# Three steps of a fused attention and two-layer kernel: the weights' conversion pieces issued behind the copies of the first sums

## The chip, the cores and the metric

The kernel runs on one core of a Trainium2 chip. Its time is that of the device, in microseconds (us), from the first to the last instruction of the one core with what lies around them. Three runs of the kernel before gave 1049.48, 1050.41 and 1051.83 us; their median, 1050.41 us, is the time to compare with.

The engines are named as in the profile: PE multiplies matrices (PEld loads its stationary operand), ACT is the scalar engine, DVE the vector engine, POOL the GpSimd engine, SP the queue that issues the DMAs. Each engine takes its instructions strictly in the order in which they were issued to it, and waits where an instruction needs something that is not there yet.

## The reference

Clustered attention over 2 batches, 8 heads and 768 positions gives `x` of 1536 rows by 512. Then come two feed-forward layers; the change lies in the first of them:

```
def _moe_ref(x, w_in, w_out):            # x 1536x512, w_in 512x2048, w_out 2048x512
    h = x @ w_in
    g = np.where(h > 0.0, h, 1.0 * (np.exp(np.minimum(h, 0.0)) - 1.0))
    return (g @ w_out).astype(np.float32)

def _moe2_ref(x, domain_probs, w1, w2):  # four experts, w1 4x512x1024, w2 4x1024x512
    p = domain_probs / (domain_probs.sum(-1, keepdims=True) + 1e-09)
    out = np.zeros((N, D), dtype=np.float32)
    for e in range(E):
        h = np.maximum(x @ w1[e], 0.0)
        out += p[:, e:e + 1] * (h @ w2[e])
    return out.astype(np.float32)
```

## The kernel before

**Products in parts.** Every fp32 operand is kept as a high and a low part, and a product is three matmuls: high by high, high by low, low by high. A weight of layer one has to be converted into these two parts before its first use.

**Steps of layer one.** The 2048 hidden columns are cut into 16 chunks of 128, and the 1536 rows into three blocks (tb) of 512. `steps` lists pairs of a block and a chunk. The chunks come in groups of 2, 4, 5 and 5, and within a group all chunks are done for block 0, then for block 1, then for block 2. So steps 0 to 5 take chunks 0 and 1 (0, 1 for block 0, 2, 3 for block 1, 4, 5 for block 2), and steps 6 to 9 take chunks 2, 3, 4 and 5 for block 0. Chunk 2 is met first in step 6, chunk 3 in step 7, chunk 4 in step 8, chunk 5 in step 9; chunk 6 only in step 18.

**What a step does.** `emit_G1(s)` is the first product: 12 matmuls (L753) into PSUM bank `h0` or `h1` (by the parity of s), then ELU: ACT makes `r` (L760, L761), DVE makes `gg` from `r` and the bank (L762), and POOL makes its high and low part `gh`, `gl` (L763, L764). The bank is free for the first product of step s + 2 when L762 of step s has read it. `emit_G2(s)` is the second product: 12 matmuls (L923), three for each of four 128-column sums. The four sums of a group of chunks stay in PSUM until the group ends; then ACT copies them out if it is the block's first group (L939, four copies, at the end of steps 1, 3 and 5) and DVE adds them to the accumulator otherwise (L941). The sums rotate through five PSUM banks: in the step that opens the next group, the first sum has a free bank, and the second sum's three matmuls wait for the first of the four copies.

The loop runs two steps ahead: iteration s issues `emit_G1(s + 2)`, then `emit_G2(s)`. PE thus goes G1(s+2), G2(s), G1(s+3), G2(s+1), and so on.

**Conversion of a chunk.** `w_split(n)` is a generator; each call of `tick` moves every running generator on by one piece. The pieces of one chunk, with one yield behind each group:

| piece | ACT | DVE | POOL |
|---|---|---|---|
| 1 | L710 (abs of the high word, to `wa`) | | |
| 2 | L716 (sign, to `wsg`) | L712, L715 | |
| 3 | | L718 (joins the low word) | |
| 4 | L722 | | |
| 5 | | L724 (times `wsg`) | |
| 6 | L726 (the high part, `wh`) | | L729 (the low part, `wl`) |

There is one buffer `wsg` for all chunks, so L716 of a chunk waits until L724 of the chunk before has read it. The raw words lie in two buffers `st`; the DMA for a chunk waits until L718 and L716 of the chunk two before are done. `tick` is called twice in an iteration of layer one, with 2s ahead of the products and with 2s + 1 behind them. A new chunk starts every 3 ticks (chunks 2 to 5) or every 4, so two chunks are under way at a time.

What sets the order on each engine is only the order in which this loop calls things. In what follows, "step s" also names iteration s of the loop.

Of the kernel before, what the change touches and what calls it, by code (L numbers as in the profile page):

```python
# [46 lines left out]
def kernel(  # L47
# [538 lines left out]
    groups, chunks, steps = [], [], []  # L586
# [37 lines left out]
    def w_load(n, raw=None, half=None):  # L624
        ly, f = chunks[n]
        if raw is None:
            t = moe_p["st"].tile([128, 2, 512, 2], I32, tag="st", name="st")
            raw = [t[:, 0], t[:, 1]]
            st_t[n] = t
        if ly == 1:  # L630
            for i, a in enumerate(raw):
                if half == 1 or i == 1:
                    src = w_out.bitcast(I32)[f * 128:(f + 1) * 128, :]
                    sp.dma_start(out=a.rearrange("p f t -> p (f t)"), in_=src)
                else:
                    src = w_in.bitcast(I32)[:, f * 256:(f + 1) * 256].rearrange("(k p) f -> p k f", p=128)
                    sp.dma_start(out=a.rearrange("p (k f) t -> p k (f t)", k=KD), in_=src)
            if half is not None:
                st_t[n] = raw[0]
        else:  # L640
            e, f = divmod(f, F2 // 256)
            f = slice(f * 256, (f + 1) * 256)
            a, b = (x.bitcast(F32).rearrange("p f t -> p (f t)") for x in raw)
            sp.dma_start(
                out=a.rearrange("p (k f) -> p k f", k=KD), in_=w1[e][:, f].rearrange("(k p) f -> p k f", p=128)
            )
            sp.dma_start(
                out=b.rearrange("p (c d) -> p c d", c=2), in_=w2[e][f, :].rearrange("(c p) d -> p c d", p=128)
            )
# [41 lines left out]
    def w_split(n, tmp=None, half=None):  # L691
        if chunks[n][0] == 2:
            yield from w2_split(n)
            return
        a = st_t.pop(n)
        if n not in w_t:
            w_t[n] = w_tiles(n)
        h, l = w_t[n]
        if half is not None:
            h, l = h[:, half], l[:, half]  # L700

        small = tmp is not None
        a32, sg = tmp if small else [gtile(("qh", "kl", "kh")[n % 3], "wa", [128, 2, 512], I32), gtile("ql", "wsg", [128, 2, 512], I32)]
        at = (slice(None),) * (len(a.shape) - 1)
        hi, lo = a[at + (1,)], a[at + (0,)]
        x, sg = a32.bitcast(F32), sg.bitcast(F32)

        act.activation(out=x, in_=hi.bitcast(F32), func=AF.Abs)  # L710
        yield
        dve.tensor_scalar(x, x, LOW, TOP, ALU.max, ALU.min)  # L712
        if small:
            yield
        dve.tensor_scalar(a32, a32, 3, 0x40000000, ALU.logical_shift_left, ALU.bitwise_xor)  # L715
        act.activation(out=sg, in_=hi.bitcast(F32), func=AF.Sign)  # L716
        yield
        dve.scalar_tensor_tensor(  # L718
            out=a32, in0=lo, scalar=29, in1=a32, op0=ALU.logical_shift_right, op1=ALU.bitwise_or
        )  # L720
        yield
        act.activation(out=x, in_=x, func=AF.Abs)  # L722
        yield
        dve.tensor_tensor(out=x, in0=x, in1=sg, op=ALU.mult)  # L724
        yield
        act.activation(out=h, in_=x, func=AF.Copy)  # L726
        if small:
            yield
        pool.tensor_tensor(l, x, h.bitcast(F32), ALU.subtract)  # L729
        yield  # L730

    def moe():
# [172 lines left out]
        def emit_G2(s, ms=range(4)):  # L905
            ly, tb, n, opens, closes, first, final = steps[s]
            if opens and 0 in ms:
                for m in range(4):
                    a_ps[m] = ps_a.tile([128, 512], F32, tag="a", name="a")
            if first and opens and 0 in ms:  # L910
                acc[tb] = accp.tile([128, 4, 512], F32, tag=f"acc{tb}", name="acc")
            for m in ms:
                ps, t, col = a_ps[m], acc[tb][:, m], slice(m * 128, (m + 1) * 128)
                ops = []
                for i, (gh, gl) in enumerate(g_t[s]):
                    if ly == 1:
                        wh, wl = w_t[n]
                        ops += [(wh[:, 1, col], gh), (wh[:, 1, col], gl), (wl[:, 1, col], gh)]
                    else:
                        wh, wl = (z[:, i] for z in w_t[n][1])  # L920
                        ops += [(gh[:, col], wh), (gh[:, col], wl), (gl[:, col], wh)]
                for i, (x, y) in enumerate(ops):
                    pe.matmul(ps, lhsT=x, rhs=y, start=(opens and i == 0), stop=(closes and i == len(ops) - 1))  # L923
                if ly == 1 or not closes:
                    continue
                i = 4 * tb + m
                e = chunks[n][1] // (F2 // 256)
                pr = prob[:, i, e:e + 1]
                if first:
                    dve.tensor_scalar(out=t, in0=ps, scalar1=pr, scalar2=None, op0=ALU.mult)  # L930
                else:
                    dve.scalar_tensor_tensor(out=t, in0=ps, scalar=pr, in1=t, op0=ALU.mult, op1=ALU.add)  # L932
                if final:
                    bb, tt = divmod(i, T)
                    sp.dma_start(out=out[bb * S:(bb + 1) * S, :].rearrange("(p t) d -> t p d", t=T)[tt], in_=t)
            if ly == 1 and closes:
                for m in ms:
                    if first:
                        act.activation(out=acc[tb][:, m], in_=a_ps[m], func=AF.Copy)  # L939
                    else:  # L940
                        dve.tensor_tensor(out=acc[tb][:, m], in0=a_ps[m], in1=acc[tb][:, m], op=ALU.add)  # L941
                if final:
                    x2_gen[tb] = x2_make(tb, acc[tb])
                    if tb < NB - 1:
                        going.append(x2_gen[tb])
                    else:
                        next(x2_gen[tb])

        def probs():
            t = tp.tile([128, B * T, 1], F32, tag="xs", name="ps")  # L950
            for b in range(B):
                sp.dma_start(
                    out=prob[:, b * T:(b + 1) * T, :],
                    in_=domain_probs[b * S:(b + 1) * S, :].rearrange("(p t) e -> p t e", t=T),
                )
            dve.tensor_reduce(out=t, in_=prob, axis=AX.X, op=ALU.add)
            dve.tensor_scalar(out=t, in0=t, scalar1=1e-9, scalar2=None, op0=ALU.add)
            dve.reciprocal(out=t, in_=t)
            dve.tensor_tensor(out=prob, in0=prob, in1=t.to_broadcast([128, B * T, E]), op=ALU.mult)


        NS1 = NS - NB * NP
# [24 lines left out]
        def tick(t, k=1):  # L987
            for n in start.get(t, ()):
                w_gen2[n] = w_split(n)
                going.append(w_gen2[n])  # L990
            for _ in range(k):
                going[:] = [it for it in going if next(it, 0) is None]
            for n in load_at.get(t, ()):
                w_load(n)
# [5 lines left out]
        def ready(s):  # L1000
            for it in (x2_gen[steps[s][1]], w_gen2[steps[s][2]]):
                for _ in it:
                    pass

        for s in range(-LAG, NS):


            nxt = s + (1 if s >= NS1 else LAG)
            q = None
            if s < NS1:  # L1010
                tick(2 * s)
            if nxt < NS1:
                emit_G1(nxt)
            elif nxt < NS and s != NS1 - 1:
                ready(nxt)
                q = quad_early(nxt)
            if s >= 0:
                emit_G2(s, (0,) if q else range(4))
            if s < NS1:
                tick(2 * s + 1)  # L1020
            if q:
                quad_late(nxt, *q)
                if s >= NS1:
                    tick(2 * s, 3)
                    tick(2 * s + 1, 2)
                emit_G2(s, (1, 2, 3))
            g_t.pop(s, None)
            if s == 12:
                probs()

    attention()
    moe()


# [28 lines left out]
```

## Time and profile before

| what | value |
|---|---|
| median of three runs | 1050.41 us (1049.48 to 1051.83) |
| the profiled execution, its time | 1049.74 us |
| the profiled execution, its span | 1048.0 us |
| PE matmul busy | 1030.3 us, 98% of the span |
| DVE, ACT, POOL busy | 735.5, 524.4, 393.3 us |
| mean granted TensorE clock | 0.997 |

The span runs from the first to the last instruction; the other 1.7 us of the execution's time lie around it. A matmul's busy time in the profile is longer than its share of the array, since matmuls overlap: 12 matmuls of 512 columns take 2.72 us from the first's start to the next group's start. So what a stall costs is read from the starts of matmuls, not from PE's busy share. Layer one begins at 269.58 us of the span (first L753) and its last L753 ends at 525.2 us; steps 0 to 9 lie between 275 and 330 us.

### The profile page before, as it was taken

The numbers are of one execution on the slowest core, as the hardware profiler recorded it, in microseconds if no ns is written. First come the engines' busy times: TensorE is split into PE (matmuls) and PEld (weight loads), VectorE is DVE, ScalarE is ACT, GpSimd is POOL, SyncE is SP. The second block draws the span as 40 slices with busy tenths as digits, with TensorE's granted clock in tenths as the row PEclk, the third lists the DMA queues.
The fourth block names the chain that finished last, engine by engine and source line by source line (L and its number), as shares of the span: only waits on it lengthen the run. The fifth ranks groups of instructions, "written<-read, shape, count | busy, mean of one in ns | idle before, by whom it ended". The sixth has DMA issues, their size and how long they took to land.

```text
span 1048.0 us, 16483 instructions
## 1 busy us (share of the span) xinstructions
PE 1030.3 (98%) x6272; PEld 920.8 (88%) x6272; DVE 735.5 (70%) x1248; ACT 524.4 (50%) x1081; POOL 393.3 (38%) x394
## 2 busy tenths in 40 slices
PE   8999999999999999999999999999999999999998
PEld 7989999989877888888888898999999898989997
DVE  6999999898689674326576765666666767666665
ACT  4989999888776563324443332233332333332331
POOL 2888888989678766344641000000000000000000
PEclk8999999999999999999999999999999999999999
DMA  7846654430323221010002101111101111001003
GB/s 171 200 104 159 143 133 113 114 91 12 136 96 122 81 95 67 1 41 1 0 1 81 41 1 41 41 41 42 40 2 41 41 41 41 15 27 41 1 1 120
DMA packets 61790, 67.53 MB, mean 64 GB/s; under 512 B 29008, under 2 KB 47440, under 8 KB 61712
## 3 DMA queue, kind: packets, MB, share of 16 engines
q1 hardware_dynamic: 61712, 66.49, 22.4%
q8 instruction: 49, 0.80, 0.3%
q14 instruction: 29, 0.24, 0.1%
HBM read 43.08 MB, written 3.15 MB: 44 GB/s over the span
## 4 chain that ended last, share of the span: by engine, by line
PE 82%; DVE 8%; ACT 4%; POOL 3%; issue 2%; DMA 0%; DVEq 0%; POOLq 0%; ACTq 0%; SPq 0%
PE a L923 35%; PE h L773 23%; PE h L753 10%; PE x L445 4%; PE tps L412 4%; PE s L364 2%; PE s L367 2%; POOL p L400 2%; DVE pl L433 2%; DVE nm L373 1%; DVE wa L718 1%; PE qkps L199 1%; ACT ph L425 1%; PE lps L239 1%; PE lps L240 1%
## 5 line engine op out<-in xcount | busy, mean ns | idle before, releaser
L773 PEld LDWEIGHTS h<-x,w1op 128*128 128x128 f32 x2016 | 257.5, 191 | 10.2 <-ACT r L784 1.2
L773 PE MATMUL h<-x,w1op 128*128 128x256 f32 x2016 | 261.2, 285 | 1.0 <-ACT r L784 1.0
L923 PE MATMUL a<-w2op,gh 128*128 128x512 f32 x768 | 238.5, 392 | 0.0
L923 PEld LDWEIGHTS a<-w2op,gh 128*128 128x128 f32 x768 | 138.1, 188 | 23.8
L932 DVE SCALAR_TENSOR_TENSOR acc<-a,prob,acc 128x512 f32<-128x512 f32 x180 | 129.7, 747 | 40.2 <-PE a L923 40.2
L923 PE MATMUL a<-w2op,gl 128*128 128x512 f32 x384 | 149.9, 390 | 0.0
L753 PE MATMUL h<-xT,wh 128*128 128x512 f32 x384 | 118.5, 390 | 0.6 <-DVE gg L762 0.6
L400 POOL TENSOR_SCALAR p<-e,sm 128x768 f32<-128x768 f32 x96 | 89.0, 933 | 40.8 <-DVE sm L394 31.0
L762 DVE SCALAR_TENSOR_TENSOR gg<-r,h 128x512 f32<-128x512 f32 x48 | 32.9, 685 | 96.5 <-ACT r L761 75.3
L373 DVE TENSOR_REDUCE nm<-s 128x1 f32<-128x768 f32 x96 | 90.8, 946 | 2.8 <-PE s L367 2.6
L382 ACT ACTIVATE e<-s,nm 128x768 f32<-128x768 f32 x96 | 86.6, 902 | 4.4 <-POOL p L400 3.2
L412 PE MATMUL tps<-ident,p 128*128 128x128 f32 x576 | 83.8, 277 | 3.2 <-DVE pl L433 3.0
L753 PEld LDWEIGHTS h<-xT,wh 128*128 128x128 f32 x384 | 71.9, 188 | 16.1 <-DVE gg L762 1.5
L784 ACT ACTIVATE r<-h 128x256 f32<-128x256 f32 x48 | 18.4, 384 | 134.8 <-PE h L773 134.8
L923 PEld LDWEIGHTS a<-w2op,gl 128*128 128x128 f32 x384 | 72.2, 188 | 15.6
L433 DVE TENSOR_TENSOR pl<-tps,ph 128x512 fp32r<-128x512 f32 x112 | 76.2, 683 | 6.6 <-ACT ph L425 5.0
L760 ACT ACTIVATE r<-h 128x512 f32<-128x512 f32 x48 | 28.6, 596 | 97.7 <-PE h L753 96.9
L445 PE MATMUL x<-ph,v 128*128 128x256 f32 x288 | 76.5, 298 | 0.1
L923 PE MATMUL a<-gh,wh 128*128 128x512 f32 x192 | 75.0, 391 | 1.0 <-ACT acc L939 0.9
L763 POOL TENSOR_SCALAR gh<-gg 128x512 fp32r<-128x512 f32 x48 | 41.0, 854 | 92.0 <-DVE gg L762 91.1
L923 PE MATMUL a<-gl,wh 128*128 128x512 f32 x192 | 74.9, 390 | 0.0
L753 PE MATMUL h<-xT,wl 128*128 128x512 f32 x192 | 74.8, 389 | 0.0
(152 smaller groups left out, 1948.4 us busy)
## 6 DMA issues: line engine op xcount, KB each, us to landing
st<-in_moe_w_dram SPq DMA_DIRECT2D x32, 512.0 KB, 4.3
st<-in_moe_w_in_dram SPq DMA_DIRECT2D x14, 512.0 KB, 3.7
st<-in_moe_w_out_dram SPq DMA_DIRECT2D x14, 512.0 KB, 4.6
QA<-qh SPq DMA_DIRECT2D x32, 192.0 KB, 3.6
nq<-in_q_dram SPq DMA_DIRECT2D x16, 192.0 KB, 3.8
nk<-in_k_dram SPq DMA_DIRECT2D x16, 192.0 KB, 3.9
nv<-in_v_dram SPq DMA_DIRECT2D x8, 384.0 KB, 3.9
QB<-ql SPq DMA_DIRECT2D x16, 192.0 KB, 3.9
```

The source lines that it names most:

```text
L373: dve.tensor_reduce(out=m_t[w][:, i:i + 1], in_=s_t[HALF * w + i][:, :, 0:384], axis=AX.XY, op=ALU.max, negate=True)
L382: act.activation(out=e, in_=s_t.pop(u)[:, :, 0:384], func=AF.Exp, bias=m_t[w][:, i:i + 1], accum_out=e_t[w][0][:, i:i + 1])
L400: pool.tensor_scalar(p, e_t[w][1 + i].rearrange("p a b -> p (a b)"), e_t[w][0][:, i:i + 1], 1.0, ALU.mult, ALU.mult)
L412: pe.transpose(ps[:, x, :], p_t[w][i][:, c * 128:(c + 1) * 128], ident)
L433: dve.tensor_tensor(out=l, in0=ps, in1=h.bitcast(F32), op=ALU.subtract)
L445: pe.matmul(x_t[w], lhsT=v2[j][:, r, c, :], rhs=t[:, :, c, :], start=(c == 0 and t is ph[w]), stop=(c == T - 1 and t is pl[w]),)
L753: pe.matmul(ps, lhsT=w[:, 0, f], rhs=x, start=(kk == 0 and i == 0), stop=(kk == KD - 1 and i == 2))
L762: dve.scalar_tensor_tensor(out=gg, in0=r, scalar=-1.0, in1=ps, op0=ALU.add, op1=ALU.max)
L763: pool.tensor_scalar(gh, gg, 1.0, 0.0, ALU.mult, ALU.add)
L773: pe.matmul(ps, lhsT=w[wz][kk], rhs=x[xz][:, kk], start=(start and kk + i == 0), stop=(stop and kk == 1 and i == 2), skip_group_check=True,)
L923: pe.matmul(ps, lhsT=x, rhs=y, start=(opens and i == 0), stop=(closes and i == len(ops) - 1))
L932: dve.scalar_tensor_tensor(out=t, in0=ps, scalar=pr, in1=t, op0=ALU.mult, op1=ALU.add)
```

## The change

In a tuple of `steps`, entry 4 says that the step closes its group of chunks and entry 5 that the group is the first. Both hold in steps 1, 3 and 5 alone, the steps whose second products end with the four copies. In these three iterations `tick(2 * s)` moves from ahead of both products to behind the second product and its copies; `tick(2 * s + 1)` follows it at once.

```diff
@@ -1007,7 +1007,9 @@
 
             nxt = s + (1 if s >= NS1 else LAG)
             q = None
-            if s < NS1:
+
+            late = 0 <= s < NS1 and steps[s][4] and steps[s][5]
+            if s < NS1 and not late:
                 tick(2 * s)
             if nxt < NS1:
                 emit_G1(nxt)
@@ -1016,6 +1018,8 @@
                 q = quad_early(nxt)
             if s >= 0:
                 emit_G2(s, (0,) if q else range(4))
+            if late:
+                tick(2 * s)
             if s < NS1:
                 tick(2 * s + 1)
             if q:
```

PE's and SP's orders stay as they are, up to buffer numbers. On ACT, DVE and POOL pieces of chunks 3 to 6 change places with the work of the first products of steps 3, 5 and 7 and with the copies.

ACT in iterations 3 and 4, before. `wh_4575` is the high part of chunk 4; the L710 and L716 ahead of it belong to chunk 5, the L722 behind it to chunk 5 and the L710 behind that to chunk 6. The first pair L760, L761 is that of step 5, the second that of step 6, and the copies are those of step 3.

```order
L722 ACTIVATE wa<-wa 128x1024
L710 ACTIVATE wa<-st 128x1024
L716 ACTIVATE wsg<-st 128x1024
L760 ACTIVATE r<-h 128x512
L761 ACTIVATE r<-r 128x512
L939 ACTIVATE acc<-a 128x512 x4
L726 ACTIVATE wh_4575<-wa 128x1024
L722 ACTIVATE wa<-wa 128x1024
L710 ACTIVATE wa<-st 128x1024
L760 ACTIVATE r<-h 128x512
```

And with the change (`wh_4613` is now the high part of chunk 4):

```order
L722 ACTIVATE wa<-wa 128x1024
L710 ACTIVATE wa<-st 128x1024
L760 ACTIVATE r<-h 128x512
L761 ACTIVATE r<-r 128x512
L939 ACTIVATE acc<-a 128x512 x4
L716 ACTIVATE wsg<-st 128x1024
L726 ACTIVATE wh_4613<-wa 128x1024
L722 ACTIVATE wa<-wa 128x1024
L710 ACTIVATE wa<-st 128x1024
L760 ACTIVATE r<-h 128x512
```

L716 of chunk 5 has gone from ahead of step 5's L760 to behind the copies. What follows it on ACT, down to step 6's L760, keeps its order.

DVE in iterations 3 and 4, before. `gg_4644`, `gg_4693` and `gg_4743` belong to steps 4, 5 and 6; `wa_4577` is chunk 4, `wa_4670` chunk 5.

```order
L762 SCALAR_TENSOR_TENSOR gg_4644<-r_4643,h_4628 128x512
L724 TENSOR_TENSOR wa_4577<-wa_4577,wsg_4578 128x1024
L712 TENSOR_SCALAR wa_4670<-wa_4670 128x1024
L715 TENSOR_SCALAR wa_4670<-wa_4670 128x1024
L762 SCALAR_TENSOR_TENSOR gg_4693<-r_4692,h_4677 128x512
L718 SCALAR_TENSOR_TENSOR wa_4670<-st_4571,wa_4670 128x1024
L762 SCALAR_TENSOR_TENSOR gg_4743<-r_4742,h_4727 128x512
```

And with the change (`gg_4689` is step 5's, `wa_4615` is chunk 4):

```order
L762 SCALAR_TENSOR_TENSOR gg_4644<-r_4643,h_4628 128x512
L762 SCALAR_TENSOR_TENSOR gg_4689<-r_4688,h_4673 128x512
L724 TENSOR_TENSOR wa_4615<-wa_4615,wsg_4616 128x1024
L712 TENSOR_SCALAR wa_4670<-wa_4670 128x1024
L715 TENSOR_SCALAR wa_4670<-wa_4670 128x1024
L718 SCALAR_TENSOR_TENSOR wa_4670<-st_4571,wa_4670 128x1024
L762 SCALAR_TENSOR_TENSOR gg_4743<-r_4742,h_4727 128x512
```

L724 of chunk 4 and L712 and L715 of chunk 5 now stand behind step 5's L762, right ahead of chunk 5's L718.

POOL in iterations 4 to 6, the difference. The first L764 is that of step 5; the pairs L763, L764 behind it are those of steps 6 and 7; `wl_4576` (now `wl_4614`) is chunk 4's low part, `wl_4669` chunk 5's.

```order
 L764 TENSOR_TENSOR gl<-gg,gh 128x512
-L729 TENSOR_TENSOR wl_4576<-wa,wh_4575 128x1024
+L729 TENSOR_TENSOR wl_4614<-wa,wh_4613 128x1024
+L763 TENSOR_SCALAR gh<-gg 128x512
+L764 TENSOR_TENSOR gl<-gg,gh 128x512
 L763 TENSOR_SCALAR gh<-gg 128x512
 L764 TENSOR_TENSOR gl<-gg,gh 128x512
 L729 TENSOR_TENSOR wl_4669<-wa,wh_4668 128x1024
-L763 TENSOR_SCALAR gh<-gg 128x512
-L764 TENSOR_TENSOR gl<-gg,gh 128x512
```

Chunk 5's L729 stood between the pairs of steps 6 and 7; it now stands behind both. (In iteration 5 its L726 has gone behind step 7's L760, L761 and step 5's copies on ACT, and chunk 6's L718 behind step 7's L762 on DVE.)

## Rows read from the trace of the kernel before

**Rows 1.** Waits, 265 to 345 us: who waited for whom, us, times, longest.

```profile
ACT wa L722 <- DVE wa L718: 8.8, 6, 2.8
...
PE a L923 <- ACT acc L939: 0.9, 1, 0.9
...
PE h L753 <- DVE gg L762: 0.6, 1, 0.6
```

**Rows 2.** Chain that ended last, 255 to 345 us: start, us, what.

```profile
315.82 3.01 PE h L753 x12
...
321.64 2.72 PE h L753 x12
```

**Rows 3.** Timeline of PE, steps 3 and 4: start, us, line, out<-in, count [idle before].

```profile
294.09 0.39 PE L923 MATMUL a<-gh,wh 128*128 128x512 f32 x1
...
300.39 0.40 PE L923 MATMUL a<-gh,wl 128*128 128x512 f32 x1
301.71 0.50 PE L923 MATMUL a<-gh,wh 128*128 128x512 f32 x1 [0.92 <-ACT acc L939]
```

**Rows 4.** Timeline of PE, in step 9's first product and at step 7's second.

```profile
316.40 0.39 PE L753 MATMUL h<-xT,wl 128*128 128x512 f32 x1
...
318.67 0.39 PE L923 MATMUL a<-gh,wh 128*128 128x512 f32 x1
```

**Rows 5.** Timeline of ACT, around steps 1, 3 and 4.

```profile
285.03 1.06 ACT L722 ACTIVATE wa<-wa 128x1024 f32<-128x1024 f32 x1 [1.01 <-DVE wa L718]
...
297.38 1.15 ACT L710 ACTIVATE wa<-st 128x1024 f32<-128x1024 f32 x1
298.87 1.16 ACT L716 ACTIVATE wsg<-st 128x1024 f32<-128x1024 f32 x1 [0.33 <-DVE wa L724]
299.93 0.58 ACT L760 ACTIVATE r<-h 128x512 f32<-128x512 f32 x1
...
301.08 2.04 ACT L939 ACTIVATE acc<-a 128x512 f32<-128x512 f32 x4
...
303.94 1.08 ACT L722 ACTIVATE wa<-wa 128x1024 f32<-128x1024 f32 x1
...
305.90 0.62 ACT L760 ACTIVATE r<-h 128x512 f32<-128x512 f32 x1
```

**Rows 6.** Timeline of DVE, around steps 1 to 5.

```profile
288.97 1.34 DVE L724 TENSOR_TENSOR wa<-wa,wsg 128x1024 f32<-128x1024 f32 x1
290.23 1.11 DVE L712 TENSOR_SCALAR wa<-wa 128x1024 f32<-128x1024 f32 x1
291.38 1.67 DVE L715 TENSOR_SCALAR wa<-wa 128x1024 int32<-128x1024 int32 x1
293.07 3.31 DVE L718 SCALAR_TENSOR_TENSOR wa<-st,wa 128x1024 int32<-128x1024 int32 x1
...
301.88 1.22 DVE L718 SCALAR_TENSOR_TENSOR wa<-st,wa 128x1024 int32<-128x1024 int32 x1
307.29 0.69 DVE L762 SCALAR_TENSOR_TENSOR gg<-r,h 128x512 f32<-128x512 f32 x1 [4.19 <-ACT r L761]
...
310.17 1.67 DVE L715 TENSOR_SCALAR wa<-wa 128x1024 int32<-128x1024 int32 x1
```

**Rows 7.** Timeline of POOL, around steps 0 to 7.

```profile
283.95 1.53 POOL L763 TENSOR_SCALAR gh<-gg 128x512 fp32r<-128x512 f32 x1 [2.05 <-DVE gg L762]
285.56 1.30 POOL L764 TENSOR_TENSOR gl<-gg,gh 128x512 fp32r<-128x512 f32 x1
286.81 2.41 POOL L729 TENSOR_TENSOR wl<-wa,wh 128x1024 fp32r<-128x1024 f32 x1
...
292.54 2.76 POOL L729 TENSOR_TENSOR wl<-wa,wh 128x1024 fp32r<-128x1024 f32 x1
...
321.98 3.39 POOL L729 TENSOR_TENSOR wl<-wa,wh 128x1024 fp32r<-128x1024 f32 x1
```

**Rows 8.** Windows: busy us of each engine, then PEclk, the granted clock.

```profile
10.00:20.00 10.00, 9.72 (x57) 9.05 (x57) 5.03 (x19) 2.27 (x7) 1.00 (x1) 0.66 0.96 210
```

## Prediction

> **What bounds the kernel now.** I read the table of waits first, then the chain that ended last, then the timelines of the engines where the three steps lie. From 321.64 us on the chain is PE alone, one product in 2.72 us [rows 2]: nothing that the change touches can gain there. The stretch to look at ends at that point. The waits in it that stop PE are small: 0.9 us for a copy (L939) and 0.6 us for a `gg` (L762); the long one, 8.8 us in six pieces, is ACT's L722 waiting for DVE's L718, which stops PE only through what is queued behind it [rows 1]. PE's starts give the whole loss: step 3's second product starts at 294.09 and step 7's at 318.67, which is 24.58 us for eight products that take 8 x 2.72 = 21.76, so 2.82 us are lost, and 0.25 us more up to 321.64 (2.97 us for one product) [rows 2 to 4]. Together 3.07 us, 0.29% of the time: more than that the change cannot gain, and 0.2% (2.1 us) is about what a measurement can tell from no change.
>
> One of the stalls is the copies': step 4's second sum starts at 301.71 where the matmul ahead of it started at 300.39; at 2.72 / 12 = 0.227 us a matmul that is 1.09 us late [rows 3]. The reader should see on ACT why: step 5's L760 could read its bank when step 3's second product began, at 294.09, but it started at 299.93, behind L716 of chunk 5, which waited for DVE's L724; the copies came at 301.08 [rows 5].
>
> **A price needed first: DVE against POOL.** The same L718 takes 1.22 us once and 3.31 us another time [rows 6]. The long one began at 293.07, while POOL's L729 ran from 292.54 to 295.30 [rows 7], and ended at 296.38, 1.08 us behind it. L729 too takes 2.41 or 3.39 us [rows 7]. So in this kernel conversion pieces of DVE and POOL do not overlap: the second waits for the first and then does nearly its whole work. The Trainium skill says so in a rule (SBUF — State Buffer, "SBUF: two separate sides"): the port pair that the vector engine and GpSimd share is an exclusive lock, held for the whole instruction, and the loser blocks fully. By that rule L718 costs its 3.31 us wherever a POOL piece is ahead of it; by the short row alone it would cost 1.22, and the sum below would come out 2.1 us smaller, at +4.0. The rule speaks against this change, since it puts DVE pieces where POOL is at work; the rows agree with it.
>
> **Step 1: nothing.** L722 of chunk 3 and L710 of chunk 4 go behind L760, L761 and the copies. Before, ACT stood idle for 1.01 us up to 285.03, waiting for DVE [rows 5]. L760 and L761 of step 3 fill that hole, the copies (2.04 us less their overlap, 1.9) end at about 287.1, and L722 ends at 288.15, so L724 of chunk 3 can start 0.8 us earlier than its 288.97. But POOL's L729 of chunk 2 runs to 289.22 (286.81 + 2.41) [rows 7], and both L724 end 1.08 us behind that, at 290.3 [rows 6]. From there the engines stand as before.
>
> **Step 3: the copies' stall goes, a longer one comes.** Without L716 of chunk 5 ahead of it, step 5's L760 follows L710, which takes about 1.0 us of ACT's queue (L722 and L710 together 303.94 to 305.90, 1.96): 297.38 + 1.0 = 298.4 instead of 299.93. The copies come as much earlier, 299.5 instead of 301.08, and PE's second sum, which followed the first copy by 0.63 us, is no longer held. Gain: 1.09 us and about 0.1 us that PE needs to start again, 1.2 us.
>
> The price is on DVE. L762 of step 5 follows its L760 by 1.39 us (305.90 to 307.29) [rows 5, 6], so at 299.8, and L724 of chunk 4 now stands behind it: 300.4, ending at 301.6 with 1.22 us. Before it had ended at 298.87, where L716 was released [rows 5]. Behind L724 come L712, L715 and L718 of chunk 5. The same four met POOL's L763, L764 and L729 in the same order for chunks 3 and 4: L724 ended at 290.31 and L718 at 296.38, 6.07 us later [rows 6, 7]. Here L763 and L764 of step 5 and L729 of chunk 4 (its L726 follows L716 on ACT, at about 302.6) are the same company, so L718 of chunk 5 ends at 301.6 + 6.07 = 307.7; before, 301.88 + 1.22 = 303.10. That is 4.6 us later.
>
> Behind it on ACT wait L722 of chunk 5, L710 of chunk 6 and then step 6's L760, which PE needs: 307.7 + 1.96 = 309.7; L762 at 311.1, done at 311.75. It frees the bank for step 8's first product. When would PE come for it? From the second sum at 301.71 there are 9 + 12 + 12 = 33 matmuls up to it, 7.5 us, and 0.1 for the restart: 309.3 before; without the copies' stall 308.1. So PE stands for about 3.5 us; less the 1.2 us gained, step 3 alone costs 2.3 us at this place.
>
> **Step 5: the weights of chunk 5 come too late.** Step 6's L762 is at 311.1 instead of 307.29. The DVE pieces behind it (L724 of chunk 5, L712 and L715 of chunk 6) ended 4.55 us after its start (310.17 + 1.67 - 307.29) [rows 6], so now at 315.65, and step 7's L762, now right behind them, ends at 316.3. POOL does L763 and L764 of step 7 next: 1.53 and 1.30 us with L718 of chunk 6 in their way, as for step 2 (283.95 to 286.81) [rows 7], from 316.4 to 319.3. Only then comes L729 of chunk 5, which stood ahead of them before. DVE's L724 of chunk 6 is there too by then (on ACT, L726 of chunk 5 and L722 of chunk 6 follow the copies), so I take the long duration, 3.39: 322.6. The third matmul of step 9's first product is the first to read `wl` of chunk 5. It started at 316.40 [rows 4]; now at 322.5. No more is added behind it: chunks 2 to 5 are then all converted and chunk 6 is met nine steps later, and the rest of the product and the next restart as they did before.
>
> SP's DMAs keep their order; their waits (L718, L716 of the chunk two before) move with the pieces, and the next load, chunk 6's, still waits for L718 and L716 of chunk 4, which do not move.
>
> **Sum.** 322.5 - 316.4 = +6.1 us: it holds the gain at the copies and the stall at step 8 already, since both lie ahead. The profiled execution took 1049.74 us, 0.67 below the median, so 1055.8 by it and 1056.5 by the median; I say 1056.0. Bounds: with the short L718 (1.22, DVE getting its turn ahead of L729: 305.6, 2.1 us earlier) and the short L729 (2.41, 1.0 earlier) +3.0 remains, 1052.7 to 1053.4. With POOL's L763 and L764 both some 0.3 us longer and slower restarts of PE, +6.9, 1056.6 to 1057.3.
>
> **The rivals.**
> *The conversion has room (faster).* Had it, all 3.07 us could come back: 1046.7 to 1047.3. It decides at L718 of chunk 5: it must end by 304.1 for PE not to wait at step 8, 1.0 us later than before, and L729 of chunk 5 by 313.3 (316.40 - 3.07). For it speaks that L718 has taken 1.22 us; against it, that even so it ends at 305.6, and that POOL's two pieces of step 7 now stand ahead of L729. Chance 0.04.
> *The pieces are hidden after all (no change).* They are moved on engines that are not full, and PE's order stays. 1049.5 to 1051.5, if stall and gain happen to cancel; the small slack of both points speaks against it. Chance 0.04.
> *Only one of the stalls.* Step 3's alone gives +2.3, the lower bounds +3.0: 1052.0 to 1053.4. DVE's turn at L718 decides, since L715 ends only some 0.5 us behind L729's start. Chance 0.09.
> *The clock falls as well.* Between 10 and 20 us the granted clock's mean is 0.66 [rows 8], that is 6.8 us at the lower of its two levels, 1.2 GHz, in the prologue with its small matmuls. Such a fall behind one of the two new stalls, each 3.5 to 4 us long, would cost half of 6.8, 3.4 us more: 1059.4. The profile has no stall of PE as long as these in a dense stretch, so neither fall nor none is shown. Chance 0.10. The Trainium skill has it as a rule (TensorE: Matmul & The Clock Gate, "HAM oscillation — how this bites in real kernels"): an idle gap of PE that is long enough sends its clock back to half rate. No run here has shown that yet.
>
> **How the numbers follow.** The forecast case has 0.73, with 1054.5 to 1057.3 as its own range. The range goes from 1052.6, which takes in half of the one-stall case, to 1059.5, which takes in about half of the clock's; some 2 in 10 are left out. Slower by over 0.2%: 0.73 + 0.09 + 0.10 less a little of the one-stall case, 0.91; within 0.2%: 0.05; faster: 0.04.
>
> **What would show it.** Right: L760 of step 5 near 298.4 and no PE wait for L939; L718 of chunk 5 ending near 307.5; a PE wait of some 3.5 us for L762 ahead of step 8's first product; a PE wait of some 4 us for POOL's L729 in step 9's; 322.5 for its third matmul, and the same course as before from there, 6 us later. Wrong: L718 of chunk 5 at 1.2 us, L729 of chunk 5 done before PE asks for it, or a granted clock below 1.0 behind 308 us.

## The result

The change makes the kernel slower: 1058.36 us median (1057.19 to 1060.13, six runs) against 1051.72 us for the kernel before in as many runs. These two medians lie 6.64 us apart (1.0063); the ratio on record is 1.0075 with a 95% interval of 1.0065 to 1.0085, that is 7.9 us. A second measurement of the same kernel gave 1.0077, with medians 8.10 us apart, which speaks for the larger figure. The profiled execution took 1058.37 us with a span of 1056.6 us.

Layer one's first matmul starts at 270.37 us in this execution and at 269.58 in that of before (first the line of before, then that of after):

```profile
269.58 0.63 PE L753 MATMUL h<-xT,wh 128*128 128x512 f32 x2
```

```profile
270.37 0.63 PE L753 MATMUL h<-xT,wh 128*128 128x512 f32 x2
```

This 0.79 us lies ahead of everything that the change touches: in the ten profiles of this study that start lies anywhere from 268.86 to 273.59. From it to the end of the span it is 786.23 us, before 778.42: +7.81 us. Comparisons of places below take the 0.79 us off.

The table of waits of the kernel after, 265 to 345 us (us, times, longest):

```profile
PE h L753 <- POOL wl L729: 3.7, 1, 3.7
PE h L753 <- DVE gg L762: 3.5, 1, 3.5
```

PE's wait for the copies (0.9 us in [rows 1]) is gone. In the place of the 0.6 us for `gg`, which lay ahead of step 9, there is one of 3.5 us ahead of step 8, and one of 3.7 us for POOL's L729 has appeared. PE's timeline has both:

```profile
312.53 0.74 PE L753 MATMUL h<-xT,wh 128*128 128x512 f32 x2 [3.53 <-DVE gg L762]
...
318.90 0.73 PE L753 MATMUL h<-xT,wh 128*128 128x512 f32 x2
323.32 0.50 PE L753 MATMUL h<-xT,wl 128*128 128x512 f32 x1 [3.69 <-POOL wl L729]
...
325.60 1.05 PE L753 MATMUL h<-xT,wh 128*128 128x512 f32 x2
...
330.06 0.62 PE L753 MATMUL h<-xT,wh 128*128 128x512 f32 x2
```

Step 8's first product starts at 312.53 after 3.53 us of idle time. Step 9's starts at 318.90 with the two matmuls that need only the high part, and its third matmul comes at 323.32. Counted from the start of layer one that is 52.95 us, against 316.40 - 269.58 = 46.82 before [rows 4]: +6.13 us. Step 10's first product starts at 330.06, 6.74 us later; before it was 5.08 us from the third matmul to there, at 321.48:

```profile
321.48 0.62 PE L753 MATMUL h<-xT,wh 128*128 128x512 f32 x2
```

The matmuls in between show why: a pair takes 1.05 us at 325.60, where it takes 0.62 at 330.06. The windows name it (their columns as in [rows 8]; the number behind POOL's count is the granted clock):

```profile
312.00:320.00 8.00, 7.01 (x26) 4.58 (x26) 6.21 (x7) 6.33 (x10) 5.89 (x5) 1.00 0.16 56
320.00:324.00 4.00, 0.68 (x3) 0.59 (x4) 2.94 (x4) 3.93 (x5) 4.00 (x2) 1.00 0.60 220
324.00:325.00 1.00, 1.00 (x5) 0.82 (x4) 0.97 (x2) 0.00 (x0) 0.92 (x2) 0.69 0.00 0
325.00:326.00 1.00, 1.00 (x3) 0.74 (x3) 1.00 (x1) 0.00 (x0) 1.00 (x2) 0.50 0.00 0
326.00:327.00 1.00, 1.00 (x4) 0.78 (x3) 1.00 (x1) 0.00 (x0) 1.00 (x1) 0.50 0.00 0
327.00:328.00 1.00, 1.00 (x5) 0.77 (x3) 0.05 (x1) 0.85 (x2) 1.00 (x1) 0.61 0.00 0
```

PE stood for most of 320 to 323.3 us; the clock was still granted in full there, fell to the lower of its two levels (1.2 GHz) at about 324.4 and came back at about 327.8. What was not granted in the four windows is 0.31 + 0.50 + 0.50 + 0.39 = 1.70 us. Behind the first wait, from 312.53 on, it stayed at 1.00. So 6.13 us up to the third matmul and 1.66 us (6.74 - 5.08) behind it make 7.79 of the 7.81 us. From 330.06 on the two executions do not differ beyond the rounding of their spans.

The chain on ACT, DVE and POOL behind the two waits, of the kernel after:

```profile
299.20 0.58 ACT L760 ACTIVATE r<-h 128x512 f32<-128x512 f32 x1
...
300.35 2.04 ACT L939 ACTIVATE acc<-a 128x512 f32<-128x512 f32 x4
...
310.44 0.58 ACT L760 ACTIVATE r<-h 128x512 f32<-128x512 f32 x1
```

```profile
305.14 3.30 DVE L718 SCALAR_TENSOR_TENSOR wa<-st,wa 128x1024 int32<-128x1024 int32 x1
311.79 0.69 DVE L762 SCALAR_TENSOR_TENSOR gg<-r,h 128x512 f32<-128x512 f32 x1 [3.35 <-ACT r L761]
...
316.26 0.68 DVE L762 SCALAR_TENSOR_TENSOR gg<-r,h 128x512 f32<-128x512 f32 x1
```

```profile
304.59 2.77 POOL L729 TENSOR_TENSOR wl<-wa,wh 128x1024 fp32r<-128x1024 f32 x1
...
319.87 3.40 POOL L729 TENSOR_TENSOR wl<-wa,wh 128x1024 fp32r<-128x1024 f32 x1
```

Step 5's L760 has come forward and the copies with it. L718 of chunk 5 began at 305.14 behind POOL's L729 of chunk 4 (304.59 to 307.36), took 3.30 us and ended at 308.44; L722 and step 6's L760 stand behind it on ACT. L729 of chunk 5 began at 319.87, behind both POOL pieces of step 7, took 3.40 us and released PE at 323.27.

### The profile page after: what moved, and what is told of

Its sections match the earlier page's. It is cut to its first block, busy times and chain, and to the rows that moved or that the text cites. A ratio compares the mean times of both kernels' runs of the same rounds, so it can differ in the third digit from the quotient of the medians.

```text
span 1056.6 us, 16483 instructions
## 1 busy us (share of the span) xinstructions
PE 1031.3 (98%) x6272; PEld 920.0 (87%) x6272; DVE 735.8 (70%) x1248; ACT 525.1 (50%) x1081; POOL 393.2 (37%) x394
## 4 chain that ended last, share of the span: by engine, by line
PE 79%; DVE 7%; POOL 5%; ACT 4%; issue 2%; SPq 1%; DMA 0%; DVEq 0%; POOLq 0%; ACTq 0%
PE a L923 35%; PE h L773 23%; PE h L753 10%; PE x L445 3%; PE tps L412 3%; POOL p L400 2%; PE s L364 1%; DVE pl L433 1%; PE s L367 1%; DVE nm L373 1%; DVE wa L718 1%; ACT e L382 1%; ACT ph L425 1%; POOL xT L477 1%; DVE wa L724 1%
## 5 line engine op out<-in xcount | busy, mean ns | idle before, releaser
L762 DVE SCALAR_TENSOR_TENSOR gg<-r,h 128x512 f32<-128x512 f32 x48 | 32.9, 686 | 102.4 <-ACT r L761 81.2
L760 ACT ACTIVATE r<-h 128x512 f32<-128x512 f32 x48 | 28.7, 597 | 105.4 <-PE h L753 104.6
L763 POOL TENSOR_SCALAR gh<-gg 128x512 fp32r<-128x512 f32 x48 | 41.9, 872 | 100.4 <-DVE gg L762 100.4
```

The lines of the kernel that those rows point to most:

```text
L762: dve.scalar_tensor_tensor(out=gg, in0=r, scalar=-1.0, in1=ps, op0=ALU.add, op1=ALU.max)
L763: pool.tensor_scalar(gh, gg, 1.0, 0.0, ALU.mult, ALU.add)
```

## The experiments

Two theories stood against each other at the start. The first: the change costs time through new waits of PE, in step 3 through L718 of chunk 5 and in step 5 through L729's place in POOL's queue, and the lower clock behind the waits adds to that. The second: moving anything behind the copies delays the conversion, whichever piece it is; the lower clock is not a matter of the waits. For each run the time from layer one's first matmul to the end of the span stands beside the ratio, here called the stretch. The stretch comes from the one profiled execution of a kernel; two executions of the changed kernel gave 786.23 and 786.20 us, and the kernel with step 1's pieces moved alone 778.25 against 778.42 before. The ratio carries the noise of the whole kernel.

### One step at a time

```diff
-            late = 0 <= s < NS1 and steps[s][4] and steps[s][5]
+            late = s == 3
```

and the same with 5 and with 1. Step 3 alone:

> Only step 3's pieces go behind the copies. Theory (a chain of waits through DVE and POOL): L718 of chunk 5 takes 3.3 us behind POOL's L729 and ends some 5 us later than before, PE waits about 3.5 us for L762 ahead of step 8's first product; L729 of chunk 5 keeps its place ahead of step 7's POOL pieces, so no wait for it in step 9. The copies of step 5 come late and hold step 6's second sum about 1 us. Sum +3.6 us, ratio 1.0035. Rival (the stall at step 8 is covered by slack further on): under +1 us, 1.001. If the lower clock came from one stall of this length alone, the granted clock falls behind 312 us and up to 1.6 us more are lost.

Measured: ratio 1.0037 (1.0025 to 1.0049); from layer one's start 782.11 us, +3.69. Its waits and windows:

```profile
PE h L753 <- DVE gg L762: 3.9, 2, 3.5
```

```profile
320.06 0.73 PE L753 MATMUL h<-xT,wh 128*128 128x512 f32 x2 [0.43 <-DVE gg L762]
```

```profile
312.00:314.00 2.00, 1.73 (x6) 1.40 (x7) 2.00 (x3) 0.62 (x1) 1.54 (x2) 0.79 0.17 70
314.00:316.00 2.00, 2.00 (x7) 1.54 (x6) 1.97 (x2) 2.00 (x3) 1.90 (x2) 0.50 0.00 0
316.00:318.00 2.00, 2.00 (x9) 1.64 (x8) 1.97 (x2) 1.97 (x5) 2.00 (x1) 0.86 0.00 0
```

There is the wait ahead of step 8, 3.5 us (the other 0.4 us of the row is ahead of step 9), and none for L729. The clock fell behind this wait and 0.42 + 1.00 + 0.28 = 1.7 us were not granted, yet the sum forecast without it holds, +3.6 expected and +3.69 measured. PE, slow matmuls and all, still waits 0.43 us for `gg` ahead of step 9, and from that product's start (320.06) to the end of the span it is 732.1 us, before 732.2 (from 315.82). So the slow matmuls only filled time in which PE would have stood. The wait of about 1 us for step 5's copies, expected in step 6, is not among PE's rows; that fits, but no execution without the fall shows it.

Step 5 alone:

> Only step 5's pieces go behind the copies. Theory: up to 308 us all is as before, the copies' 1.1 us wait in step 4 included; L729 of chunk 5 stands behind step 7's L763 and L764 and PE waits some 3.5 us for it in step 9's first product, the small waits at steps 6 and 9 of before go. Sum +2.5 us, ratio 1.0024. Rival (L729 is late only because step 3 made everything late): no wait for L729, a gain of under 1 us, ratio 0.999 to 1.000. If one stall of this length is enough for the clock to fall, up to 1.6 us more.

Measured: ratio 1.0035 (1.0022 to 1.0048); from layer one's start 782.47 us, +4.05.

```profile
PE h L753 <- POOL wl L729: 3.4, 1, 3.4
```

```profile
318.46 0.64 PE L753 MATMUL h<-xT,wl 128*128 128x512 f32 x1 [3.44 <-POOL wl L729]
```

```profile
318.00:320.00 2.00, 1.54 (x4) 1.24 (x5) 1.95 (x2) 1.10 (x2) 1.92 (x3) 0.67 0.00 0
320.00:322.00 2.00, 2.00 (x6) 1.51 (x6) 1.98 (x1) 0.00 (x0) 2.00 (x2) 0.50 0.00 0
322.00:324.00 2.00, 2.00 (x10) 1.64 (x9) 0.19 (x1) 1.31 (x3) 2.00 (x1) 0.98 0.27 60
```

The wait for L729 is there without step 3's, so it does not come from step 3's delay; the rival falls. The clock fell behind it (0.66 + 1.00 + 0.04 = 1.7 us), where no wait hides it: layer one starts at 269.23 us here, so the third matmul comes 2.41 us later than before (49.23 against 46.82 us; 2.5 expected), and the other 1.64 of the 4.05 us lie behind it.

Step 1 alone:

> Only step 1's pieces go behind the copies. Theory: L724 of chunk 3 can start earlier but POOL's L729 of chunk 2 holds it until the same moment as before, so both run alike from L712 of chunk 4 on: 0 us, ratio 1.000. Rival (any step's pieces behind the copies delay the conversion): +1 us or more, 1.001.

Measured: ratio 0.9999 (0.9988 to 1.0009), from layer one's start 778.25 us, -0.17. Step 1 costs nothing.

### The clock: work for PE where it would stand

```diff
+        def filler(n):
+            wh, xh = w_t[2][0], xT[0][0][:, 0]
+            ps = ps_h.tile([128, 512], F32, tag="h2", name="fill")
+            for i in range(n):
+                pe.matmul(ps, lhsT=wh[:, 0, 0:128], rhs=xh, start=True, stop=True)
...
+            if nxt in (8, 9):
+                filler(14)
             if nxt < NS1:
                 emit_G1(nxt)
```

> The change, with 14 matmuls of 512 columns (3.2 us) ahead of each of the first products of steps 8 and 9, into the PSUM bank that layer one leaves free; their results are not read. They fill the time in which PE would stand. Theory (the two stalls let the clock fall, which costs about 1.5 us behind the second one): the third matmul of step 9's first product starts when it did with the change, the granted clock stays at 1.00 behind it, and the kernel is about 1.5 us faster than with the change alone: +6.1 us against before, ratio 1.0058. Rival (the slow matmuls behind the second stall have nothing to do with PE standing still): they stay slow, ratio 1.0073 to 1.0078. If the filler delays the products itself, more than 1.008.

Measured: ratio 1.0063 (1.0048 to 1.0078); from layer one's start 784.51 us, +6.09 against before and 1.7 us less than with the change alone. PE and the windows:

```profile
273.59 0.63 PE L753 MATMUL h<-xT,wh 128*128 128x512 f32 x2
...
321.85 3.34 PE L1004 MATMUL fill<-xT,wh 128*128 128x512 f32 x14
...
326.54 0.50 PE L753 MATMUL h<-xT,wl 128*128 128x512 f32 x1 [0.90 <-POOL wl L729]
```

```profile
308.00:316.00 8.00, 7.66 (x34) 6.07 (x33) 4.62 (x4) 3.19 (x4) 2.72 (x2) 1.00 0.38 130
316.00:324.00 8.00, 7.97 (x34) 5.97 (x34) 6.21 (x6) 7.14 (x11) 6.52 (x5) 1.00 0.20 56
324.00:332.00 8.00, 7.10 (x32) 5.56 (x31) 6.32 (x7) 5.95 (x9) 7.92 (x4) 1.00 0.25 91
```

Layer one starts at 273.59 us here, so the third matmul comes at 326.54 - 273.59 = 52.95 us: to the hundredth where the change has it. The filler delayed nothing, PE waited 0.9 us instead of 3.7, the clock stayed, and what was lost behind the wait is gone: from the third matmul to the end of the span it is 731.56 us, before 731.60, with the change alone 733.28. The ratios of the two kernels overlap in their intervals; it is the stretch from layer one's start, one execution with the filler against two without, that tells them apart.

The change a second time:

> The change once more, for a second look at the clock. Theory: stalls of 3.5 and 3.7 us at the same places, and the granted clock falls behind one of the two, not always the same, since it did so behind the second in the change's profile and behind the only one in those of step 3 alone and step 5 alone. Rival (the fall behind the second stall belongs to that place): it falls there again and never behind the first. Ratio 1.0075 either way, 1.006 where it does not fall.

Measured: ratio 1.0077 (1.0062 to 1.0092), from layer one's start 786.20 us.

```profile
312.54 0.72 PE L753 MATMUL h<-xT,wh 128*128 128x512 f32 x2 [3.52 <-DVE gg L762]
...
319.73 0.61 PE L753 MATMUL h<-xT,wh 128*128 128x512 f32 x2
323.38 0.50 PE L753 MATMUL h<-xT,wl 128*128 128x512 f32 x1 [3.03 <-POOL wl L729]
```

```profile
312.00:314.00 2.00, 1.46 (x5) 1.19 (x6) 2.00 (x3) 0.34 (x1) 1.35 (x1) 0.88 0.33 135
314.00:316.00 2.00, 2.00 (x6) 1.55 (x5) 1.97 (x2) 1.97 (x4) 1.70 (x2) 0.50 0.00 0
316.00:318.00 2.00, 2.00 (x8) 1.59 (x8) 2.00 (x3) 2.00 (x6) 0.91 (x1) 0.77 0.00 0
...
322.00:324.00 2.00, 0.62 (x2) 0.58 (x3) 1.84 (x3) 2.00 (x3) 2.00 (x2) 0.94 0.11 45
324.00:326.00 2.00, 2.00 (x6) 1.51 (x6) 1.97 (x2) 0.01 (x1) 1.92 (x3) 0.50 0.00 0
326.00:328.00 2.00, 2.00 (x8) 1.58 (x7) 1.10 (x1) 0.45 (x1) 2.00 (x2) 0.71 0.00 0
```

The waits are 3.52 and 3.03 us, and the clock fell behind both; behind the first it had not in the other execution. The total is the same 786.2 us. The slow matmuls bring step 9's first product later, 7.19 us behind step 8's where it was 6.37, but the wait behind it is shorter (3.03 us instead of 3.69), and the third matmul comes at 323.38 - 270.40 = 52.98 us, where it was 52.95: L729's end does not depend on them. So a fall behind the first wait costs nothing, while the one behind the second costs its 1.6 to 1.7 us (from the third matmul to the end 733.22 us, before 731.60). Expected was one fall at a changing place; there were two, and the rival, which bound it to the second place alone, falls too.

### What POOL has to do with it

```diff
-        pool.tensor_tensor(l, x, h.bitcast(F32), ALU.subtract)
+        if n in (4, 5):
+            dve.tensor_tensor(out=l, in0=x, in1=h.bitcast(F32), op=ALU.subtract)
+        else:
+            pool.tensor_tensor(l, x, h.bitcast(F32), ALU.subtract)
```

> The change, with L729 of chunks 4 and 5 on DVE instead of POOL. Theory (the time goes to DVE and POOL shutting each other out, and to L729's place in POOL's queue): L718 of chunk 5 no longer meets L729, the stall ahead of step 8 shrinks from 3.5 to about 2.5 us, the wait for the low part of chunk 5 in step 9 from 3.7 to under 1 us; +3.4 us, ratio 1.0032. Rival (only the order on DVE and ACT counts, and the two subtractions make DVE's queue longer): both stalls stay, ratio 1.006 to 1.009.

Measured: ratio 1.0047 (1.0033 to 1.0060); from layer one's start 781.29 us, +2.87. Waits, PE's first product of step 8, a window and DVE's timeline (the lines lie three further down from L730 on, where DVE's subtraction stands: L765 is `gg`, L756 the first product):

```profile
PE h L756 <- DVE gg L765: 2.5, 1, 2.5
...
PE a L926 <- POOL gl L767: 0.4, 1, 0.4
```

```profile
310.89 0.73 PE L756 MATMUL h<-xT,wh 128*128 128x512 f32 x2 [2.45 <-DVE gg L765]
```

```profile
310.00:315.00 5.00, 4.11 (x11) 3.24 (x12) 4.82 (x5) 3.01 (x6) 3.04 (x2) 0.66 0.20 83
```

```profile
304.45 1.21 DVE L730 TENSOR_TENSOR wl<-wa,wh 128x1024 fp32r<-128x1024 f32 x1
305.59 1.21 DVE L718 SCALAR_TENSOR_TENSOR wa<-st,wa 128x1024 int32<-128x1024 int32 x1
```

L718 of chunk 5 takes 1.21 us where it took 3.30, and the subtraction ahead of it 1.21 where POOL took 2.77. L718 ends 36.99 us behind layer one's start, with the change 38.07, and by the same 1.08 us the wait ahead of step 8 is shorter, 2.45 us (2.5 expected). The one for L729 is gone from PE's rows, and a small one for `gl` of step 9 has come. The ratio lies above the 1.0032 expected and the stretch, at 1.0027 of the whole, below it; a fall of the clock behind the wait belongs to this profile too (granted 0.66 in the mean from 310 to 315 us, 1.7 us withheld), and the profiled execution, 1052.87 us, is among the shorter of the six (1052.36 to 1056.89). Which of the two is nearer stays open; both lie well under the change's 1.0075 and its +7.8 us.

### Which of the two chunks: a version that gains

In these iterations of layer one each tick moves the two chunks under way on. Here the older one's piece stays ahead of the products and the younger one's goes behind the copies:

```diff
+        def older(t):
+            for n in start.get(t, ()):
+                w_gen2[n] = w_split(n)
+                going.append(w_gen2[n])
+            rest = going[1:]
+            going[:] = [it for it in going[:1] if next(it, 0) is None]
+            return rest
+
+        def younger(t, rest):
+            going.extend(it for it in rest if next(it, 0) is None)
+            for n in load_at.get(t, ()):
+                w_load(n)
...
-            if s < NS1:
+            split_tick = s in (1, 3, 5)
+            if split_tick:
+                rest = older(2 * s)
+            elif s < NS1:
                 tick(2 * s)
...
+            if split_tick:
+                younger(2 * s, rest)
             if s < NS1:
                 tick(2 * s + 1)
```

> In steps 1, 3 and 5 alone, the older chunk's piece stays ahead of the products and only the younger chunk's goes behind the copies. Theory (the older chunk's pieces carry the whole cost of the change): no wait for L729 in step 9, at most 0.2 us for L762 ahead of step 8, the copies' wait of step 4 gone but one of about 1 us at step 6; -0.6 us, ratio 0.9995. Rival (the younger chunk's L712, L715 and L716 behind step 5's L762 are what makes L718 late): a wait of 2 us or more ahead of step 8, ratio 1.002 or more.

Measured: ratio 1.0007 (0.9993 to 1.0021); from layer one's start 777.84 us, -0.58. The waits of this kernel that stop PE:

```profile
PE a L923 <- ACT acc L939: 0.9, 1, 0.9
```

No wait of PE for `gg` or for L729 is left in the table, and the copies' wait has only moved, as expected. By the stretch it is the -0.6 us expected; by the ratio it is no change. The younger chunk's pieces behind the copies cost nothing, so the change's whole cost comes only once the older one's go there too; the older one's alone were not run.

The same with `split_tick = s < 6`, that is in iterations -2 to 5:

> The kernel before, in which in iterations -2 to 5 the first tick moves only the older of the two chunks under way ahead of the products and the younger one behind them and the copies. Theory (the loss of the change is that the older chunk's pieces, L724, L726 and L729, go behind the work of the next first product, while its gain is that the younger chunk's L710, L716, L712, L715 and L718 do): the wait for L939 in step 4 and those for L762 ahead of steps 6 and 9 go, nothing new comes, -2.7 to -3.0 us, ratio 0.9973. Rival (any piece moved behind the copies delays the weights of chunks 4 and 5): a wait of PE for L729 or L762 of 2 us or more, ratio 1.000 to 1.004.

Measured: 1046.67 us median (1045.97 to 1047.94), ratio 0.9968 (0.9956 to 0.9979), 3.4 us faster than the kernel before; from layer one's start 775.51 us, -2.91. The chain through the stretch:

```profile
270.85 8.19 PE h L753 x36
...
322.56 2.72 PE a L923 x12
```

From layer one's first matmul to 345 us PE has no wait left here: every product takes 2.72 us, and no row of the waits from 265 to 345 us has PE's matmuls waiting for ACT, DVE or POOL. By the starts of PE's matmuls that is all that could be gained (2.91 us, see below). It beats both kernels.

## Where the prediction was right, and the step that failed

**What bounds, and step 1: right.** The place of the loss and step 1's zero hold. The 3.07 us to be gained are 0.16 too many: they were read up to 321.64, where the chain passes to step 10's first product, but its first matmul starts at 321.48 in the timeline above. From start to start the loss is 2.82 + 0.09 = 2.91 us, and the last version gains just that.

**Step 3 and step 5: right in mechanism and nearly to the tenth.** With 0.79 taken off: step 5's L760 at 298.41 (298.4 said), the copies at 299.56 (299.5), L718 of chunk 5 ending at 307.65 (307.7), step 6's L762 at 311.00 (311.1), the wait 3.53 us (3.5), step 7's L762 ending at 316.15 (316.3), L729 of chunk 5 at 3.40 us (3.39) and the third matmul at 322.53 (322.5). The sum to that point, +6.1 us, is 6.13. It hung on the choice of the long durations for L718 and L729, taken from rows with the same neighbours; the short ones would have given +3.0. That L718 is long because of POOL is shown by the run with L729 on DVE.

**The step that failed** is the sentence "No more is added behind it", by which the rest of the product and the next restart go as they did before: the sum put nothing behind step 9's third matmul. Behind the second wait the clock fell to its lower level, and 1.66 us were added there. The prediction names a granted clock below 1.0 behind 308 us as a sign of being wrong, and this sign came. The fall itself was among the rivals, at a chance of 0.10 and a price of 3.4 us, taken from the long fall in the prologue [rows 8]. Both were wrong. All five profiles with a wait of PE of 2.4 us or more show a fall: four behind each such wait (step 3 alone, step 5 alone, L729 on DVE, the change again), the fifth, that of the change, behind one of two. Each fall withheld 1.70 us, half of the price, and cost that much only where no later wait of PE took it up. The filler shows the cause: with PE at work in the same time, the fall and the 1.7 us are gone. The forecast itself contained two waits longer than any in the profile of before, so the chance should have been much larger than a tenth.

The rule of the Trainium skill that the prediction cites (TensorE: Matmul & The Clock Gate, "HAM oscillation — how this bites in real kernels"), that a long enough idle gap sends the clock back to half rate, is borne out behind six of the seven such waits, of 2.45 to 3.69 us, and not behind the seventh, of 3.53 us.

**The number.** 1056.0 us was said and 1058.36 measured. The range up to 1059.5 holds it, in part by luck: its upper end takes in about half of the clock's case, at a price twice too high. As a change the sum was +6.1 us and the two profiles show +7.81; the missing part is the clock. The 1056.0 said is +5.6 us on the 1050.41 then known; by the ratio the change is 7.9 us (6.8 to 8.9), and the kernel before measured 1051.72 beside it.

**The rivals.** None of the others came: there was no room for the conversion, nothing cancelled, and both stalls appeared. The part of the first that was right shows in the last version: there was room for the younger chunk's pieces.

## What to carry to other kernels

When work is moved behind other work so that a wait ends sooner, follow each moved piece to its consumer. Here, of two chunks in the pipeline, the older had its consumer near and the younger had time: moving both in three steps cost 7.8 us, moving the younger alone there cost nothing, and moving it in eight iterations gained 2.9. A piece that is short alone can take much longer where it meets a neighbour on another engine (L718: 1.2 and 3.3 us); take its duration from a row with the same neighbours. And a new wait of the matmul engine of a few microseconds is to be priced with the slow matmuls behind it, 1.7 us here, unless another wait follows that takes them up.

## What was not expected of the hardware

The granted clock fell behind waits of PE of 2.45 us (L729 on DVE), 3.03, 3.44, 3.52, 3.52 and 3.69 us, by these windows always after PE had begun to work again, and each time 1.70 us were not granted; in one execution it did not fall behind a wait of 3.53 us, at a place where it fell in another execution of the same kernel. In the kernel before, whose longest wait in this stretch is 0.92 us, it stayed.
